# A transformer block on one core: gate and up of token tile 14 computed inside tile 15's attention, and the tail's chain in another order

## The chip, the cores and the metric

The kernel runs on 1 core of one Trainium2 chip, as one program. The metric is the device time of one execution in microseconds (us); a kernel's time is the median of several runs. The engines are named as in the profile: PE (TensorE matmul) with PEld (its weight load), DVE (VectorE), ACT (ScalarE), POOL (GpSimd) and SP (SyncE, which issues nearly all DMAs). Each engine works through its own list of instructions in order and waits at semaphores.

## The reference

```python
def _A_ref(x, wqkv, wo):                       # B, S, D = 1, 2048, 512; H = 32 heads of Dh = 16
    qkv = (x @ wqkv).reshape(B, S, 3, H, Dh)...
    scores = jnp.einsum('bhqd,bhkd->bhqk', q, k) * Dh ** (-0.5)
    p = _softmax(scores, axis=-1)
    o = jnp.einsum('bhqk,bhkd->bhqd', p, v)
    return o.transpose(...).reshape(B, S, D) @ wo
def _B_ref(x, w_gate, w_up, w_down):           # F = 1792
    return _gelu(x @ w_gate) * (x @ w_up) @ w_down
mod = (_silu(c) @ w_mod).reshape(c.shape[0], 6, 1, -1)
sa, ca, ga, sb, cb, gb = ...
h = _layernorm(x) * (1 + ca) + sa
x = x + ga * _A_ref(h, A_wqkv, A_wo)
h = _layernorm(x) * (1 + cb) + sb
x = x + gb * _B_ref(h, B_w_gate, B_w_up, B_w_down)
```

Inputs and output are bf16. The scores are 32 x 2048 x 2048, which makes the exponential the largest elementwise work.

## The kernel before, in words

The 2048 tokens are 16 tiles of 128. As queries they come in seven sets (`SETS`): two of 512 tokens, three of 256, and the last two of one tile each, tile 14 (`SETS[5]`) and tile 15 (`SETS[6]`). The 32 heads are eight quads (`qd`) of four. A unit is one set and one quad; for tiles 14 and 15 the first `QS` quads (5 before) are one unit of 256 queries for both tiles, the others are units of 128 queries for each tile alone, all of tile 14's first. A unit is worked through in rounds of four slots, one slot being 512 columns of scores of one head; there are 2048 slots in all.

The score matmuls (`qk`, `ps_sc<-qT,kme` or `kmo`) fill three PSUM banks at a time, in two alternating groups. ACT takes two or three banks at once through the exponential (`E<-ps_sc 128x1024` or `128x1536`). At times DVE takes one bank of a group instead (`bits`): it computes the exponential by bit work, a first step out of PSUM for each slot and three steps for each round of four slots (`power_task`: `mant`, `square`, `expo`, on 128x2048). Then `pv_mms` accumulates probabilities times values in the bank `ps_pv`; the values have a column of ones, which gives the softmax's sum.

At a unit's end (`unit_end`) DVE copies the accumulator to `osb`. The sums take one of two ways. By the DMA route they go through DRAM (`scr_den`), come back as `den`, DVE takes the reciprocal (`rden`), which goes out (`scr_rec`) and comes back spread over the partitions in four DMAs (`rb`). By `near_end` PE spreads the sums with a matmul against `self32` (`ps_mi<-osb,self` or `ps_sc<-osb,self`) and DVE takes the reciprocal of 128x128 in place. Either way DVE multiplies `onorm<-osb,rb`. Quads 6 and 7 of tiles 14 and 15 take the second way before the change.

Everything else is side work in PE's gaps: projections, then for each set `side_wo` (eight matmuls with `wo`, residual sum, statistics), the norm steps (`ln2_steps`) and `side_ffn` (transposes, gate, gelu, up, product, down). While the exponentials run, a side matmul with 128 columns of weights is issued as four pieces of 32 columns (`split`), which run beside one another; in the tail it is whole. The gate is copied raw from PSUM to `hreg` by DVE, and ACT does the gelu later in two long instructions, since a change between exponential and gelu needs a table load each way.

The order is set when the program is built: `stream` walks the slots with a model of the engines and writes a fixed list for each of them; `plan` gives each piece of side work a first slot and a due slot (`DUE`), and `RULES` holds nine numbers for every 128 slots that steer how side work, DVE's slots and filler matmuls (`ps_mi<-xs,ident`, `ps_pv<-xs,nil`, results unused) are put in.

After the last slot comes `tail`. Before the change two generators run in it: `tail_end` for tile 15 (last reciprocal, `wo`, statistics, norm, transposes, then `tail_ffn`), and `tail_ffn` for tile 14, all of its gate, up and down. `tail_ffn` goes by chunks of four blocks of F: gate, gelu on ACT, up, product, and the downs of the chunk before. `side_last` prepares tile 14 during tile 15's attention, up to the transposes of its normed tokens (`begin=True`). `down_fin` multiplies with `gb`, adds the residual and issues the output's DMA.

Of the kernel before, what the change touches and what calls it, by code (L numbers as in the profile page):

```python
# [6 lines left out]
ACT = mybir.ActivationFunctionType  # L7
ALU = mybir.AluOpType
# [6 lines left out]
P = 128  # L15
# [6 lines left out]
NDC = D // P  # L22
NFC = F // P
# [5 lines left out]
SETS = ((0, 512), (512, 512), (1024, 256), (1280, 256), (1536, 256), (1792, 128), (1920, 128))  # L29
OCOL = (0, 0, 0, 256, 0, 256, 384)  # L30
BCOL = (0, 0, 0, 0, 0, 0, 128)
NSET = len(SETS)
QS = 5
CH = 3
SC = 2 * CH
NSL = 27
# [6 lines left out]
FIRST = 0  # L43
LAST = 3
FLOW = 4
DUE = lambda ends: (ends[1] + 30, 1420, 1605, ends[4] + 10, ends[5] - 20)
URGENT = 12
LATE = 2
RULES = (
# [16 lines left out]
)  # L66
END = (0, None)

# [380 lines left out]
class _Kernel(_Recorder):  # L449
# [12 lines left out]
    def alloc(self):  # L462
# [6 lines left out]
        self.hT = hreg[:, :].rearrange("p (a n) -> p a n", a=NDC)  # L469
        self.prodT = hreg[:, 0:NFC * 512].rearrange("p (f n) -> p f n", f=NFC)  # L470
        self.prodL = hreg[:, 0:NFC * 256].rearrange("p (f n) -> p f n", f=NFC)
        self.tb2 = hreg[:, 0:4 * D].rearrange("p (t n) -> p t n", t=4)
        wreg = sb("wreg", [P, NDC * 1536], BF16)
        self.wqkv = wreg[:, :].rearrange("p (a n) -> p a n", a=NDC)
# [563 lines left out]
        self.done(("ffn", gi))  # L1038


    def side_last(self, k):
        sums = self.near_end(k + 1, 6, self.mi[:, 0:P])
        for y in self.side_ffn(k, True):
            yield y
            if y is END and sums is not None and ("osb", k + 1, 6) in self.have:
                yield from sums
                sums = None
        if sums is not None:
            yield from sums

    def task(self, steps, key, when=None):

# [49 lines left out]
    def plan(self, ends, nsplit):  # L1102

        def at(i):
            return i * 2.5 if i < nsplit / 2.5 else nsplit + 3 * (i - nsplit / 2.5)
        a = ends[0]
        w = [(lambda: self.side_v(0, 0), 0, at(3)), (self.side_first, 0, at(30))]
        w.append((self.side_wo_load, at(30), at(30)))
        w.append((lambda: self.side_dc(1), at(30), at(51)))
        w.append((self.side_mod, at(50), at(59)))  # L1110
        w.append((lambda: self.side_dc(2), at(59), at(90)))
        w.append((lambda: self.side_q_all(1), at(90), at(105)))
        w.append((lambda: self.side_dc(3), at(105), at(133)))
        w.append((lambda: self.side_q_all(2), at(133), at(160)))
        w.append((lambda: self.side_q_all(3), at(160), a + 40))
        n = ends[-1]
        due = DUE(ends)
        for k, e in enumerate(due):
            s0 = max(ends[k] + 33, due[k - 1] if k else 0)
            w.append((lambda k=k: self.side_wo(k), s0, min(e, s0 + 15 * SETS[k][1] // P)))  # L1120
            w.append((lambda k=k: self.side_ffn(k), s0, e))
        k, s0 = len(SETS) - 2, ends[-2] - 16
        w.append((lambda: self.near_end(k, 6, self.mi[:, 0:P]), s0, s0))
        w.append((lambda: self.near_end(k, 7, self.mi[:, 0:P]), s0, s0))
        w.append((lambda: self.side_wo(k), s0, s0))
        w.append((lambda: self.side_last(k), s0, n - 20))
        res = []
        for mk, s, e in w:
            self.dry = True
            tot = sum(y[0] for y in mk() if y is not None)  # L1130
            self.dry = False
            res.append([mk(), s, e, tot, None])
        return res
# [423 lines left out]
    def unit_end(self, u, acc):  # L1557
        sets, qd, q0, W = u
# [1 line left out]
        osb, rb = self.osb[:, lo:hi], self.rb[:, lo:hi]  # L1560
        assert not self.blocked(u)
        self.copy("dve", osb, acc[:, 0:W])
        if sets[0] >= len(SETS) - 2 and len(sets) == 1 and qd >= 6:
            self.done(("osb", sets[0], qd))
            return
        self.live[u] = (lo, hi)
# [32 lines left out]
    def tail(self, ka, kb):  # L1599

        self.split = False
        gens = [self.tail_end(kb), self.tail_ffn(ka, self.pv[:, :], range(0, 3), 0)]
        nxt = [None] * len(gens)
        while True:
            t = self.pe_now()
            while any(self.step(x, max(self.free[x], t) + 40) for x in ("act", "dve", "sp")):
                pass
            best = None
            for i, g in enumerate(gens):
                if g is None:  # L1610
                    continue
                if nxt[i] is None:
                    nxt[i] = next(g, 0)
                if nxt[i] == 0:
                    gens[i] = None
                elif nxt[i] is not None:
                    x = self.probe(nxt[i])
                    if best is None or max(x, t + 30) < best[0]:
                        best = max(x, t + 30), i
# [15 lines left out]
            f, nxt[best[1]] = nxt[best[1]], None  # L1635
            f()

    def tail_end(self, k):
        q0, W = SETS[k]
# [16 lines left out]
        for h in range(2):  # L1656
            pb = self.scp[:, 4 + h, :]
            yield lambda h=h, pb=pb: self.transp(pb, lambda t: self.normed(k, t), 1, h)
            for i in range(2):
                dc = 2 * h + i  # L1660
                self.modulate("act" if i == 0 else "dve", self.t2T[:, dc, c0:c0 + W],
                              pb.bitcast(BF16)[:, W * i:W * i + W], self.modB, dc)
        yield from self.tail_ffn(k, self.mi[:, :], (4, 5, 0, 1, 2, 3), 4)

    def tail_ffn(self, k, down, banks, e0):
        q0, W = SETS[k]
        c0, tile, kpb = BCOL[k], q0 // P, 512 // W
        chunks = [range(a, min(NFC, a + kpb)) for a in range(0, NFC, kpb)]
        nb = [0]

        def up(ci, w):
            if nb[0] == 2 and k == len(SETS) - 1:
                yield from self.until(("p", k - 1, len(chunks) - 1))
            bk = self.scp[:, banks[nb[0] % len(banks)], :]
            nb[0] += 1
            for s, fc in enumerate(chunks[ci]):
                for dci in range(NDC):
                    yield lambda s=s, fc=fc, dci=dci: self.up_mm(bk[:, W * s:W * s + W], w, fc, c0, W, dci)
            return bk
        if k < len(SETS) - 1:  # L1680
            yield from self.until(("begun", k))
            self.act(self.tcol[:, 0:1], self.tcol[:, 0:1], ACT.Gelu_apprx_tanh)
        for ci in range(len(chunks) + 1):
            if ci < len(chunks):
                n = len(chunks[ci])
                g = self.E[:, e0 + ci, 0:W * n]
                bg = yield from up(ci, self.wg)
                self.task([("act", lambda bg=bg, g=g, n=n: self.act(g, bg[:, 0:W * n], ACT.Gelu_apprx_tanh))],
                          ("g", k, ci))
                bu = yield from up(ci, self.wu)  # L1690
                yield from self.until(("g", k, ci))
                self.task([lambda bu=bu, g=g, n=n, f0=chunks[ci][0]: self.stt(
                    self.prodL[:, f0:f0 + n, c0:c0 + W], bu[:, 0:W * n].rearrange("p (k n) -> p k n", k=n), 1.0,
                    g.rearrange("p (k n) -> p k n", k=n), ALU.mult, ALU.mult)], ("p", k, ci))
            if ci:
                yield from self.until(("p", k, ci - 1))
                for fc in chunks[ci - 1]:
# [46 lines left out]
```

## Time and profile before

| | |
|---|---|
| time, median of 3 runs (lowest, highest) | 823.86 us (823.32, 823.99) |
| profiled execution | span 822.1 us from the first to the last instruction; it has no time of its own beside the span |
| ACT busy | 792.7 us, 96% |
| PE busy | 755.0 us, 92% |
| DVE busy | 753.1 us, 92% |
| granted TensorE clock, mean | 1.000 |
| DMA | 43.73 MB, 53 GB/s on the mean |

An engine's busy time is the union of its instructions' times. Matmuls are pipelined and their ends are modelled, so for their rate the distance from one group's start to the next is used, not the mean of one. In the rows of instructions in order the first number is the start and the second the length in us; a bracket at the end gives the idle time before and what ended it. In the rows by group the number behind the bar is busy time in us, then the mean of one instruction in ns, then idle time ahead of the group.

### The profile page before, as it was taken

How to read it: one execution, taken by the hardware profiler on the slowest of the kernel's cores; microseconds unless marked ns; L12 is line 12 of the kernel's file. 1: busy time of each engine (PE TensorE's matmuls, PEld its weight loads, DVE VectorE, ACT ScalarE, POOL GpSimd, SP SyncE). 2: the span in 40 equal slices, each digit the busy share in tenths (PEclk: the TensorE clock that was granted, in tenths of full speed). 3: DMA queues.
4: the chain of work that ended last, by engine and by line, in shares of the span. 5: the costliest groups of instructions: out<-in, count | busy, mean ns of one | idle time of the engine just before them, and what ended most of it. 6: DMA issues, size and time to landing. Idle time of an engine off the chain costs nothing.

```text
span 822.1 us, 30036 instructions
## 1 busy us (share of the span) xinstructions
PE 755.0 (92%) x13614; PEld 296.8 (36%) x13614; DVE 753.1 (92%) x1349; ACT 792.7 (96%) x740; POOL 4.5 (1%) x13
## 2 busy tenths in 40 slices
PE   8999999988898998999898989998899998999998
PEld 3333333322222222222233333333443344345556
DVE  7866999999999999999999999999999999689864
ACT  5999999999999999999999999999999999999982
POOL 2000000000000000000000000000000000000000
PEclk9999999999999999999999999999999999999999
DMA  8101000000003211110002322200644243420000
GB/s 273 63 2 36 9 10 10 10 10 7 4 10 98 59 47 33 46 32 22 16 20 59 87 59 57 54 26 13 174 136 123 73 124 89 126 57 10 22 7 14
DMA packets 76361, 43.73 MB, mean 53 GB/s; under 512 B 20557, under 2 KB 74634, under 8 KB 76234
## 3 DMA queue, kind: packets, MB, share of 16 engines
q1 hardware_dynamic: 76232, 41.82, 18.5%
q8 instruction: 106, 1.74, 0.9%
q14 instruction: 21, 0.17, 0.1%
q10 hardware_dynamic: 2, 0.00, 0.0%
HBM read 39.18 MB, written 2.61 MB: 51 GB/s over the span
## 4 chain that ended last, share of the span: by engine, by line
ACT 90%; PE 6%; DVE 2%; DMA 0%; issue 0%; DVEq 0%
ACT E L356 86%; PE ps_sc L337 4%; ACT hreg L356 3%; PE ps_mi L337 2%; ACT L356 1%; PE ps_pv L337 1%; DVE dreg L368 0%; DMA xs<-in_A_x_dram 0%; DVE hreg L360 0%; DVE st L396 0%; DVE mreg L368 0%; DVE wreg L360 0%; PE ps_sc L341 0%; DVE mreg L360 0%; DVE dreg L360 0%
## 5 line engine op out<-in xcount | busy, mean ns | idle before, releaser
L356 ACT ACTIVATE E<-ps_sc 128x1024 bf16<-128x1024 f32 (+2 forms) x702 | 748.2, 1295 | 11.8 <-PE ps_sc L337 11.8
L337 PE MATMUL ps_sc<-qT,kmo 32*128 32x256 bf16 (+2 forms) x1664 | 199.6, 299 | 20.7 <-ACT E L356 18.2
L337 PE MATMUL ps_sc<-qT,kme 32*128 32x256 bf16 (+2 forms) x1600 | 194.7, 304 | 23.7 <-ACT E L356 19.0
L368 DVE TENSOR_SCALAR mreg<-ps_sc 128x512 uint16<-128x512 f32 x248 | 166.3, 685 | 18.1 <-PE ps_sc L337 15.9
L337 PE MATMUL ps_pv<-E,vaug 128*17 128x256 bf16 (+2 forms) x2536 | 149.4, 300 | 0.5 <-DVE osb L377 0.2
L368 DVE TENSOR_SCALAR dreg<-ps_sc 128x512 uint16<-128x512 f32 x164 | 109.9, 684 | 4.8 <-PE ps_sc L337 3.4
L337 PE MATMUL ps_mi<-wreg,mreg 128*32 128x256 bf16 (+1 forms) x1888 | 108.3, 326 | 4.7 <-DVE hreg L360 2.0
L337 PEld LDWEIGHTS ps_sc<-qT,kme 32*128 32x128 bf16 x1600 | 53.6, 92 | 143.2 <-ACT E L356 120.9
L337 PEld LDWEIGHTS ps_sc<-qT,kmo 32*128 32x128 bf16 x1664 | 56.7, 92 | 129.5 <-ACT E L356 109.8
L337 PEld LDWEIGHTS ps_pv<-E,vaug 128*17 128x17 bf16 x2536 | 51.3, 89 | 55.6 <-issue 40.9
L368 DVE TENSOR_SCALAR mreg<-mreg 128x2048 uint16<-128x2048 uint16 x103 | 69.6, 680 | 0.2
L337 PEld LDWEIGHTS ps_mi<-wreg,mreg 128*32 128x32 bf16 x1888 | 41.0, 95 | 46.6 <-issue 19.5
L337 PE MATMUL ps_pv<-mreg,vaug 128*17 128x256 bf16 (+2 forms) x888 | 51.8, 298 | 3.4 <-DVE mreg L360 1.8
L360 DVE TENSOR_TENSOR mreg<-mreg 128x2048 bf16<-128x2048 bf16 x41 | 49.6, 1211 | 0.0
L360 DVE TENSOR_TENSOR mreg<-dreg,mreg 128x2048 bf16<-128x2048 bf16 x35 | 42.5, 1213 | 0.1
L337 PE MATMUL ps_mi<-hreg,wreg 128*32 128x512 bf16 x480 | 38.5, 384 | 1.1 <-DVE vaug L377 0.9
L360 DVE TENSOR_TENSOR hreg<-ps_mi,hreg 128x512 bf16<-128x512 f32 x47 | 32.2, 684 | 1.3 <-PE ps_mi L337 0.9
L337 PE MATMUL ps_mi<-xs,ident 128*32 128x512 bf16 (+2 forms) x416 | 32.6, 375 | 0.3 <-DVE hreg L360 0.2
L377 DVE CAST hreg<-ps_mi 128x512 bf16<-128x512 f32 x46 | 31.5, 684 | 0.7 <-PE ps_mi L337 0.2
L368 DVE TENSOR_SCALAR dreg<-dreg 128x2048 uint16<-128x2048 uint16 x47 | 32.0, 681 | 0.1
L337 PE MATMUL ps_mi<-wo,onorm 128*32 128x512 bf16 x416 | 31.7, 383 | 0.2 <-DVE qT L368 0.2
L337 PE MATMUL ps_mi<-mreg,hreg 128*32 128x512 bf16 x352 | 28.8, 384 | 0.0
(166 smaller groups left out, 680.1 us busy)
## 6 DMA issues: line engine op xcount, KB each, us to landing
mreg<-in_B_w_up_dram SPq DMA_DIRECT2D x32, 256.0 KB, 3.0
mreg<-in_B_w_gate_dram SPq DMA_DIRECT2D x28, 256.0 KB, 3.7
mreg<-in_B_w_down_dram SPq DMA_DIRECT2D x16, 256.0 KB, 3.0
dreg<-in_B_w_down_dram SPq DMA_DIRECT2D x12, 256.0 KB, 3.4
mreg<-in_w_mod_dram SPq DMA_DIRECT2D x1, 2048.0 KB, 12.7
rb<-scr_rec SPq DMA_DIRECT2D x64, 32.0 KB, 1.9
out_dram<-xs SPq DMA_DIRECT2D x16, 128.0 KB, 1.7
rb<-scr_rec SPq DMA_DIRECT2D x116, 16.0 KB, 1.8
```

Source lines behind the costliest of these rows:

```text
L337: return self.rec("pe", lambda e: e.matmul(out, lhsT, rhs, start=start, stop=stop, tile_position=tp), [lhsT, rhs, *after], [out], cost=(n, ...
L356: return self.rec("act", lambda e: e.activation(out, in_, func, scale=scale, **kw), rd, wr, cost=self.cost("act", out, [in_], "act") + load)
L360: return self.rec(eng, lambda e: e.tensor_tensor(out, a, b, op), [a, b], [out], cost=self.cost(eng, out, [a, b], "tt"))
L368: return self.rec(eng, lambda e: e.tensor_scalar(out, a, s1, s2, **kw), rd, [out], cost=self.cost(eng, out, [a], "ts") + (60 if len(rd) > ...
L377: return self.rec(eng, lambda e: e.tensor_copy(out, in_), [in_], [out], cost=self.cost(eng, out, [in_], "ts"))
```

## The change

`QS` falls to 2, so quads 2 to 7 of tiles 14 and 15 are single units. Quads 6 and 7 of tile 14 and now 5, 6 and 7 of tile 15 go by `near_end` (`PEN`). `side_last` goes on after the transposes with `side_raw`: all eight chunks of tile 14's gate and up are computed inside tile 15's attention and copied raw to `gate5` and `up5` in `hreg`. In the tail, `tail_rest` does tile 14's gelus (ACT, SBUF to SBUF), products and downs; the last two products wait for tile 15's norm. `tail_ffn`, now for tile 15 alone, does all gate chunks first, then up chunks with downs between them. The windows of side work (`WIN`, `DUE`) and ten rows of `RULES` have other numbers, so the built order differs from the last part of the 256-query sets on; ahead of slot 1000 or so it is the same.

```diff
-QS = 5
+QS = 2
+PEN = {NSET - 2: (6, 7), NSET - 1: (5, 6, 7)}
+NRAW = 8
...
-DUE = lambda ends: (ends[1] + 30, 1420, 1605, ends[4] + 10, ends[5] - 20)
+DUE = (1054, 1420, 1597, 1802, -12, 0, -20)
+def WIN(ends):
+    due = DUE[:4] + (ends[5] + DUE[4], ends[5] - 16 + DUE[5], ends[6] + DUE[6])
...
+        self.gate5 = hreg[:, 0:NFC * 256].rearrange("p (f n) -> p f n", f=NFC)[:, :, 0:P]
+        self.up5 = hreg[:, NFC * 256 + 2048:NFC * 256 + 2048 + NFC * P].rearrange("p (f n) -> p f n", f=NFC)
...
+    def raw_chunk(self, k, i, mi):
+        W, c0 = SETS[k][1], BCOL[k]
+        x, f0 = i // 4, i % 4 * 4
+        n = min(4, NFC - f0)
+        for s in range(n):
+            for dci in range(NDC):
+                yield W, lambda s=s, dci=dci: self.up_mm(
+                    mi[:, W * s:W * s + W], (self.wg, self.wu)[x], f0 + s, c0, W, dci)
+        dst = (self.gate5, self.up5)[x][:, f0:f0 + n, :]
+        return lambda eng: self.copy(eng, dst, mi[:, 0:W * n].rearrange("p (k n) -> p k n", k=n))
...
     def side_last(self, k):
-        sums = self.near_end(k + 1, 6, self.mi[:, 0:P])
-        for y in self.side_ffn(k, True):
+        sums = [(qd, self.near_end(k + 1, qd, self.mi[:, 0:P])) for qd in PEN[k + 1][:-1]]
+        for gen in (self.side_ffn(k, True), self.side_raw(k)):
...
-        if sets[0] >= len(SETS) - 2 and len(sets) == 1 and qd >= 6:
+        if len(sets) == 1 and qd in PEN.get(sets[0], ()):
...
-        gens = [self.tail_end(kb), self.tail_ffn(ka, self.pv[:, :], range(0, 3), 0)]
+        gens = [self.tail_end(kb), self.tail_rest(ka, self.pv[:, :])]
...
+    def tail_rest(self, k, down):
...
+        early, late = self.after([("onorm", last, 7)]), self.after([("ln2", last)])
+        when = (early, early, late, late)
+        for j, h in enumerate(part):
...
+            self.task([("act", lambda h=h: self.act(self.gate5[:, h, :], self.gate5[:, h, :], ACT.Gelu_apprx_tanh))], ("g5", j))
+        for j, h in enumerate(part):
...
+            self.task([lambda h=h: self.tt("dve", self.gate5[:, h, :], self.gate5[:, h, :], self.up5[:, h, :], ALU.mult)],
+                      ("p5", j), when[j])
+            yield from self.until(("p5", j))
+            for fc in range(h.start, h.stop):
+                yield lambda fc=fc: self.down_mm(down, BCOL[k] // P, fc)
+        self.task([lambda: self.down_fin(down, q0 // P)], ("fin", k), self.after([("ln2", k + 1)]))
...
-        yield from self.tail_ffn(k, self.mi[:, :], (4, 5, 0, 1, 2, 3), 4)
+        yield from self.tail_ffn(k, self.mi[:, :], (0, 1, 2, 3, 4, 5), 4)
...
+        for i in range(nc):
+            n = len(chunks[i])
+            yield from up(i, self.wg)
...
+        for i in range(nc + 1):
+            if i < nc:
+                n = len(chunks[i])
+                yield from self.until(("g", k, i))
+                yield from up(nc + i, self.wu)
...
+            if i:
+                yield from self.until(("p", k, i - 1))
+                for fc in chunks[i - 1]:
                     yield lambda fc=fc: self.down_mm(down, c0 // P, fc)
```

More of the change, by code (lines that the diff above doesn't have):

```diff
@@ L45 @@
 FLOW = 4
-DUE = lambda ends: (ends[1] + 30, 1420, 1605, ends[4] + 10, ends[5] - 20)
+DUE = (1054, 1420, 1597, 1802, -12, 0, -20)
+def WIN(ends):
+    due = DUE[:4] + (ends[5] + DUE[4], ends[5] - 16 + DUE[5], ends[6] + DUE[6])
+    res = []
+    for k in range(NSET - 2):
+        s0 = max(ends[k] + 33, due[k - 1] if k else 0)
+        res += [(s0, min(due[k], s0 + 15 * SETS[k][1] // P)), (s0, due[k])]
+    return res + [(due[5], due[5]), (due[5], due[6])]
 URGENT = 12
@@ L1038, in side_ffn, with side_raw @@
         self.done(("ffn", gi))
-    def side_last(self, k):
-        sums = self.near_end(k + 1, 6, self.mi[:, 0:P])
-        for y in self.side_ffn(k, True):
[L1044 to L1049, printed above, removed]
+    def raw_chunk(self, k, i, mi):
[8 more added lines that the diff above has]
+        return lambda eng: self.copy(eng, dst, mi[:, 0:W * n].rearrange("p (k n) -> p k n", k=n))
+    def side_raw(self, k):
+        for i in range(NRAW):
+            f = yield from self.raw_chunk(k, i, self.bank())
+            f("dve")
+            self.done(("raw", k, i))
+            yield END
+    def side_last(self, k):
+        sums = [(qd, self.near_end(k + 1, qd, self.mi[:, 0:P])) for qd in PEN[k + 1][:-1]]
+        for gen in (self.side_ffn(k, True), self.side_raw(k)):
+            for y in gen:
+                yield y
+                if y is END and sums and ("osb", k + 1, sums[0][0]) in self.have:
+                    yield from sums.pop(0)[1]
+        for _, x in sums:
+            yield from x
     def task(self, steps, key, when=None):
@@ L1116, in plan @@
         n = ends[-1]
[L1117 to L1126, printed above, removed]
+        win = WIN(ends)
+        for k in range(NSET - 2):
+            w.append((lambda k=k: self.side_wo(k),) + win[2 * k])
+            w.append((lambda k=k: self.side_ffn(k),) + win[2 * k + 1])
+        k = NSET - 2
+        for qd in PEN[k]:
+            w.append((lambda qd=qd: self.near_end(k, qd, self.mi[:, 0:P]),) + win[2 * k])
+        w.append((lambda: self.side_wo(k),) + win[2 * k])
+        w.append((lambda: self.side_last(k),) + win[2 * k + 1])
         res = []
@@ L1617, in tail @@
                     x = self.probe(nxt[i])
-                    if best is None or max(x, t + 30) < best[0]:
-                        best = max(x, t + 30), i
+                    x = max(x, t + 30), i if ("ln2", kb) not in self.have else -i
+                    if best is None or x < best[:2]:
+                        best = x + (i,)
             w = self.next_side()
@@ L1634, in tail @@
                 continue
-            f, nxt[best[1]] = nxt[best[1]], None
+            f, nxt[best[2]] = nxt[best[2]], None
             f()
+    def tail_rest(self, k, down):
+        q0, W = SETS[k]
+        for i in range(NRAW, 8):
+            gen = self.raw_chunk(k, i, self.scp[:, i % 3, :])
+            while True:
+                try:
+                    yield next(gen)[1]
+                except StopIteration as stop:
+                    f = stop.value
+                    break
+            self.task([lambda f=f: f("dve")], ("raw", k, i))
+        part = [slice(a, min(a + 4, NFC)) for a in range(0, NFC, 4)]
+        last = k + 1
+        early, late = self.after([("onorm", last, 7)]), self.after([("ln2", last)])
+        when = (early, early, late, late)
+        for j, h in enumerate(part):
+            for i in range(h.start // 4, (h.stop + 3) // 4):
+                yield from self.until(("raw", k, i))
+            self.task([("act", lambda h=h: self.act(self.gate5[:, h, :], self.gate5[:, h, :], ACT.Gelu_apprx_tanh))], ("g5", j))
+        for j, h in enumerate(part):
+            for i in range(h.start // 4, (h.stop + 3) // 4):
+                yield from self.until(("raw", k, 4 + i))
+            yield from self.until(("g5", j))
+            self.task([lambda h=h: self.tt("dve", self.gate5[:, h, :], self.gate5[:, h, :], self.up5[:, h, :], ALU.mult)],
[4 more added lines that the diff above has]
+        self.task([lambda: self.down_fin(down, q0 // P)], ("fin", k), self.after([("ln2", k + 1)]))
     def tail_end(self, k):
@@ L1668, in tail_ffn @@
         chunks = [range(a, min(NFC, a + kpb)) for a in range(0, NFC, kpb)]
[L1669 to L1676, printed above, removed]
-                for dci in range(NDC):
-                    yield lambda s=s, fc=fc, dci=dci: self.up_mm(bk[:, W * s:W * s + W], w, fc, c0, W, dci)
-            return bk
@@ L1680, in tail_ffn @@
[L1680 to L1697, printed above, removed]
+        nc = len(chunks)
@@ new lines, in tail_ffn, with up @@
+        bank = [self.scp[:, banks[i % len(banks)], :] for i in range(2 * nc)]
+        def up(i, w):
+            for s, fc in enumerate(chunks[i % nc]):
+                for dci in range(NDC):
+                    yield lambda s=s, fc=fc, dci=dci: self.up_mm(bank[i][:, W * s:W * s + W], w, fc, c0, W, dci)
+        for i in range(nc):
+            n = len(chunks[i])
+            yield from up(i, self.wg)
+            g = self.E[:, e0 + i, 0:W * n]
+            self.task([("act", lambda i=i, g=g, n=n: self.act(g, bank[i][:, 0:W * n], ACT.Gelu_apprx_tanh))], ("g", k, i))
@@ new lines, in tail_ffn @@
+        for i in range(nc + 1):
[3 more added lines that the diff above has]
+                yield from up(nc + i, self.wu)
+                g = self.E[:, e0 + i, 0:W * n]
+                self.task([lambda i=i, g=g, n=n: self.stt(
+                    self.prodL[:, chunks[i][0]:chunks[i][0] + n, c0:c0 + W], bank[nc + i][:, 0:W * n].rearrange("p (k n) -> p k n", k=n), 1.0,
+                    g.rearrange("p (k n) -> p k n", k=n), ALU.mult, ALU.mult)], ("p", k, i))
+            if i:
+                yield from self.until(("p", k, i - 1))
+                for fc in chunks[i - 1]:
```

18 rows, old and new, of the table RULES are left out of this document.

## The prediction

> **What bounds the kernel now.** I read the page first, for the shares and the chain of work that ended last.
>
> ```profile
> span 822.1 us, 30036 instructions
> PE 755.0 (92%) x13614; PEld 296.8 (36%) x13614; DVE 753.1 (92%) x1349; ACT 792.7 (96%) x740; POOL 4.5 (1%) x13
> ...
> ACT 90%; PE 6%; DVE 2%; DMA 0%; issue 0%; DVEq 0%
> ```
>
> ACT carries 90% of the chain. The profiled execution has no time of its own beside its span of 822.1; the three runs have a median of 823.86, so 1.76 us lie around the span, and I carry those over unchanged. Where ACT lets go shows in the busy time by stretches and in ACT's timeline.
>
> ```profile
> 20.00:796.30 776.30, 716.63 (x13140) 271.95 (x13132) 724.89 (x1269) 774.56 (x712) 0.31 (x1) 1.00 0.18 49
> 748.90:796.30 47.40, 44.45 (x1327) 25.22 (x1323) 39.28 (x75) 47.38 (x46) 0.00 (x0) 1.00 0.07 15
> 796.27:822.10 25.83, 22.13 (x284) 17.08 (x284) 13.83 (x33) 7.13 (x13) 0.00 (x0) 1.00 0.04 13
> ```
> ```profile
> 748.89 47.36 ACT L356 ACTIVATE E<-ps_sc 128x1024 bf16<-128x1024 f32 x45
> 796.27 1.28 ACT L356 ACT_TABLE_LOAD   x1
> 797.56 0.20 ACT L356 ACTIVATE tcol<-tcol 128x1 f32<-128x1 f32 x1
> ```
>
> The columns after the length are PE, PEld, DVE, ACT, POOL, granted clock, DMA share and GB/s. From 20 to 796.3 ACT is idle for only 1.74 us: exps end to end. At 796.27 the last exp ends, and 25.83 us of tail follow, in which PE is busy for 22.13. So the kernel is "sum of ACT until the last exp" plus "tail", and the change is costed in these two.
>
> **The exps.** Their prices, from the last stretch by form:
>
> ```profile
> L356 ACT ACTIVATE E<-ps_sc 128x1024 bf16<-128x1024 f32 x29 | 28.8, 1122 | 0.0
> L356 ACT ACTIVATE E<-ps_sc 128x1536 bf16<-128x1536 f32 x15 | 22.4, 1565 | 0.0
> ```
>
> The means overlap one another (29 x 1122 alone is 32.5), so I use them only for the difference: 1565 - 1122 = 443 ns for 512 more columns, where one wide exp's overlap may differ from a narrow one's; I take 0.425, and 0.443 moves the sum by under 0.1. Of the 45 exps in 47.36 one is of 512 columns. Then 45 exps in 47.36 give (47.36 - 14 x 0.425) / 45 = 0.920 for 1024 columns, 1.345 for 1536, 0.495 for 512. The instruction lists of the two programs have 444 exps of 1024 before and 451 after, 249 and 246 of 1536, one and none of 512 (tail gelus not counted): DVE takes 408 of the 2048 score slots after, 412 before, because it now has other work. ACT's sum rises by 7 x 0.920 - 3 x 1.345 - 0.495 = **+1.9 us**. The gelu pairs and table loads ahead of the tail are as many as before. With 1.74 us of idle in 776, nothing absorbs this; it moves the last exp.
>
> **PE and DVE under the exps.** Gate and up of tile 14 (SETS[5]) are 112 matmuls of 128 columns; in the attention each is cut into four pieces for 32 columns of weights, 448 pieces, four abreast. Narrow work of that kind, and what PE has to spare in the last stretch:
>
> ```profile
> 786.19 0.40 PE L337 MATMUL ps_pv<-E,vaug 128*17 128x128 bf16 x16
> 786.41 0.40 PE L337 MATMUL ps_pv<-dreg,vaug 128*17 128x128 bf16 x16
> 793.10 0.62 PE L337 MATMUL ps_pv<-mreg,vaug 128*17 128x128 bf16 x32
> 793.66 0.40 PE L337 MATMUL ps_sc<-qT,kmo 32*128 32x128 bf16 x12
> ```
> ```profile
> L337 PE MATMUL ps_mi<-xs,ident 128*32 128x512 bf16 x24 | 2.2, 382 | 0.0
> L337 PE MATMUL ps_pv<-xs,nil 128*17 128x128 bf16 x52 | 1.1, 220 | 0.0
> L337 PE MATMUL ps_pv<-E,vaug 128*17 128x128 bf16 x291 | 7.1, 220 | 0.1
> L337 PE MATMUL ps_pv<-E,vaug 128*17 128x256 bf16 x56 | 2.4, 274 | 0.0
> ```
>
> Sixteen pieces take 0.22 (786.19 to 786.41), so 448 take 6.2; with the switch to score matmuls included, 32 take 0.56, so 7.8 at the worst. QS falls from 5 to 2, so three quads of heads run 128 wide instead of 256: by busy time per column PV costs 7.1/(291x128) = 0.19 ns against 2.4/(56x256) = 0.17, which on 49152 columns is 1.1 us. PE thus needs 7.3 us more. It has 2.95 idle in these 47.4 us and 3.3 of fillers in the two rows above (matmuls whose result is not used): 6.3, and the last tile's own attention starts earlier than 748.9 now, because six of its eight quads are single, before three. The instruction list agrees: single-width nil fillers fall from 52 to 4. I count no loss, but the cover is thin; without it every microsecond goes straight into the exps.
>
> DVE gets eight copies of raw gate and up out of PSUM and loses four score slots and one quad's bit work:
>
> ```profile
> L368 DVE TENSOR_SCALAR mreg<-ps_sc 128x512 uint16<-128x512 f32 x12 | 8.2, 687 | 3.3 <-PE ps_sc L337 3.2
> L368 DVE TENSOR_SCALAR mreg<-mreg 128x2048 uint16<-128x2048 uint16 x7 | 4.8, 681 | 0.1
> L360 DVE TENSOR_TENSOR mreg<-mreg 128x2048 bf16<-128x2048 bf16 x3 | 3.7, 1220 | 0.0
> ```
>
> Six full copies and two halves are about 6 x 0.69 + 2 x 0.42 = 5.0; the loss is 4 x 0.69 + 2 x 0.68 + 1.22 = 5.3. That is even, and DVE has 8 us idle in the last stretch. Two more units go by the DMA route for their reciprocals, 14 more issues on SP, which is idle between them.
>
> **The tail.** Here is the chain of tile 15 (SETS[6]) before, in order of time.
>
> ```profile
> 796.73 0.29 DVE L377 COPY osb<-ps_pv 128x128 f32<-128x128 f32 x1 [0.17 <-PE ps_pv L337]
> ...
> 797.15 0.96 DVE L380 RECIPROCAL rb<-ps_mi 128x128 f32<-128x128 f32 x1
> 797.17 0.44 PE L337 MATMUL ps_sc<-osb,self 128*128 128x128 f32 x2
> ...
> 798.64 0.95 DVE L380 RECIPROCAL rb<-ps_sc 128x128 f32<-128x128 f32 x1
> ...
> 801.23 0.28 DVE L360 TENSOR_TENSOR onorm<-osb,rb 128x128 bf16<-128x128 f32 x1
> ...
> 802.04 0.81 PE L337 MATMUL ps_sc<-wo,onorm 128*128 128x512 bf16 x3
> ...
> 802.89 0.70 DVE L396 BATCH_NORM_STATS2 st<-ps_sc 128x6 f32<-128x512 f32 x1 [1.38 <-PE ps_sc L337]
> ...
> 803.72 0.67 DVE L373 SCALAR_TENSOR_TENSOR hreg<-ps_sc,E 128x512 bf16<-128x512 f32 x1
> ...
> 805.58 0.81 DVE L368 TENSOR_SCALAR E<-ps_sc,mv,rstd 128x512 bf16<-128x512 f32 x1
> ...
> 806.44 0.40 PE L341 MATMUL ps_sc<-ident,E 128*128 128x128 bf16 x4
> ...
> 807.73 1.25 PE L337 MATMUL ps_sc<-wreg,qT 128*128 128x128 bf16 x16
> 808.82 1.06 PE L337 MATMUL ps_sc<-wreg,mreg 128*128 128x128 bf16 x16
> ...
> 811.50 1.03 PE L337 MATMUL ps_mi<-xs,hreg 128*128 128x512 bf16 x4
> ...
> 812.36 1.06 PE L337 MATMUL ps_sc<-wreg,qT 128*128 128x128 bf16 x16
> ...
> 817.40 0.69 DVE L360 TENSOR_TENSOR wreg<-ps_mi,gb 128x512 bf16<-128x512 f32 x1 [0.83 <-PE ps_mi L337]
> ...
> 819.38 0.42 DVE L360 TENSOR_TENSOR xs<-xs,wreg 128x512 bf16<-128x512 bf16 x1
> ```
>
> Three delays stand in it. The last quad's reciprocal starts at 798.64 though its sum was ready at 797.61: quad 6's reciprocal (797.15) was ahead in DVE's queue. Quad 5's onorm came only at 801.23, by the DMA route, so wo waited until 802.04. And PE did tile 14's matmuls in between. After the change quads 5, 6 and 7 of the last tile all go over PE, quad 6's reciprocal is issued ahead of the last osb copy, and tile 14 keeps only gelus, products and its 14 downs.
>
> I lay out the changed order with these durations, in us after the last exp's end. osb copy 0.46 to 0.75 (796.73). Sum on PE to 1.34 (797.61). Reciprocal, at once now, 1.37 to 2.32. onorm to 2.64. One wo matmul, the seven others done: to about 3.15. Stats from 3.19. From stats to norm the old chain took 805.58 - 802.89 = 2.69, with a 0.67 product in it; now a 0.42 one (the nearest row is the bf16 product from SBUF at 819.38; at worst 0.67 as it was): 2.44, so norm 5.63 to 6.44. Transposes to 6.9. Four downs of tile 14 stand in PE's queue ahead of the gate: from 6.95 for 0.86. **Gate starts at 7.8**; before, at 11.46 (807.73).
>
> From there PE has the 112 matmuls of tile 15 (0.89 for sixteen: three groups stand from 808.82 to 811.50), 6.2, and 16 downs (0.86 for four, 811.50 to 812.36), 3.4. The output starts when the last down is through, at 17.5 after the last exp; before, at 21.1 (817.40). No wait is seen in that stretch: while a product is made, PE has the next up chunk or four downs. The output takes 0.69 for the product and 0.42 for the add, 1.2 with the gap; before, tile 14's came behind it, and the last add ended at 819.80, 23.53 after the last exp. Now at 18.7. The last DMA's 2.3 (819.80 to 822.1) stays. The tail shrinks by **4.8 us**, to 21.0. Bounds: 1.2 if only the second output goes, 6.2 if all the moved matmuls do; I take 4.8, as each step but one has its own row.
>
> [...] The row first: the table load is 1.28 long, and the next activation starts at 797.56, 1.29 after it; the first raw gelu, taken at the 0.5 of an exp of 512 columns, is then done at 1.8, well ahead of its product at 2.64. [...]
>
> **Sum.** 823.86 + 1.9 - 4.8 = **821.0**.
>
> **Rivals.** (a) *The chain does not get short.* In DVE's queue quad 4's onorm, by the DMA route, now stands ahead of quad 6's onorm and quad 7's reciprocal. The route, measured:
>
> ```profile
> 794.16 0.34 SPq L406 DMA_DIRECT2D scr_rec<-rden  x1
> 796.43 1.71 SPq L406 DMA_DIRECT2D rb<-scr_rec  x4
> ```
>
> From the reciprocal to the landing is 4.0 us; on SP it stands behind the same steps of quads 2 and 3, which wait for DVE as well. It decides once quad 4's reciprocal runs later than 3.3 us before the last exp's end. In the order eight exps follow it, 8 us, which speaks against; DVE's queue, with eight copies that wait for PE, speaks for. A delay of 2.5 gives 823.5: no change. Chance 0.17.
>
> (b) *PE becomes the bound in the last tile's attention: slower.* If the fillers stood where nothing else can, only the 2.95 idle covers, and the 448 pieces cost 7.8 with switches, PV 1.1 more: 8.9 - 2.95 = 5.9 us of ACT waits, 826.9. It gets slower than before once these waits pass 2.9 us. For it: PE was busy for 94% of that stretch. Against: ACT never waited there (idle 0.0 in all three exp rows). Chance 0.11.
>
> (c) *The clock falls in the tail*, which loses PE work. Every row shows 1.00; at half, the stretch from gate to last down takes 9.7 more: 830.7. [...] Chance 0.04.
>
> That the change does not do what it says is out: all 448 pieces stand ahead of the last score matmuls in PE's list.
>
> **Numbers.** Forecast 0.68, (a) 0.17, (b) 0.11, (c) 0.04. A difference of 0.2%, 1.65 us, is about what a measurement of this kernel can tell from none. Faster is the forecast, 0.68; same is (a), 0.17; slower is (b) and (c), 0.15. The range: low, a tail shorter by 6.2 with all of the 1.9 paid, 819.6, and 0.3 for ACT's share in the rounding of the prices, 819.3; high, the forecast with half of the 6.3 of cover missing, 3.2 more, 824.2, which also holds (a). Left out are (b) and (c), 0.15.
>
> **What would show it.** Right: the last exp ends near 798.2 with ACT idle under 3 us ahead of it, gate starts about 8 us after it, one output at the end, span about 819.2. Wrong on the exps: ACT waits for PE in the last 50 us. Wrong on the tail: an onorm that waits for a DMA, or PE waiting between up and down.

## The result, and the profile after

The changed kernel takes 829.75 us (median of 4, 827.44 to 830.77) against 823.69 before: slower, ratio 1.007 with a 95% interval of 1.0053 to 1.0087. In a second series it was 828.25, ratio 1.005 (1.0032 to 1.0068). The forecast was 821.0, in a range of 819.3 to 824.2. The profiled execution is the fastest of the first four: 827.44, span 825.7, with a mean clock of 1.000, where the three others had 0.994 to 0.998.

First the page of the changed kernel, then ACT's instructions in order at the end of the attention.

```profile
span 825.7 us, 31347 instructions
PE 753.6 (91%) x14256; PEld 303.8 (37%) x14256; DVE 754.5 (91%) x1359; ACT 795.3 (96%) x742; POOL 4.5 (1%) x13
...
q8 instruction: 111, 1.82, 0.9%
...
ACT 83%; PE 11%; DVE 2%; DMA 1%; SPq 1%; issue 1%; DVEq 0%
```
```profile
782.97 4.37 ACT L369 ACTIVATE E<-ps_sc 128x1024 bf16<-128x1024 f32 x4
788.24 2.46 ACT L369 ACTIVATE E<-ps_sc 128x1024 bf16<-128x1024 f32 x2 [0.91 <-PE ps_sc L350]
791.54 1.02 ACT L369 ACTIVATE E<-ps_sc 128x1024 bf16<-128x1024 f32 x1 [0.84 <-PE ps_sc L350]
792.77 1.45 ACT L369 ACTIVATE E<-ps_sc 128x1536 bf16<-128x1536 f32 x1 [0.21 <-PE ps_sc L350]
795.29 2.46 ACT L369 ACTIVATE E<-ps_sc 128x1024 bf16<-128x1024 f32 x2 [1.07 <-PE ps_sc L350]
799.03 3.38 ACT L369 ACTIVATE E<-ps_sc 128x1024 bf16<-128x1024 f32 x3 [1.28 <-PE ps_sc L350]
803.22 1.02 ACT L369 ACTIVATE E<-ps_sc 128x1024 bf16<-128x1024 f32 x1 [0.82 <-PE ps_sc L350]
804.26 1.28 ACT L369 ACT_TABLE_LOAD   x1
805.56 1.97 ACT L369 ACTIVATE hreg<-hreg 128x512 bf16<-128x512 bf16 x4
```

PE's share of the chain went from 6% to 11%. The last exp ends at 804.26; before it was 796.27, the forecast 798.2. The brackets say what ACT did in between: six waits for score matmuls in 20 us, 5.1 us in all. The tail behind the last exp is 825.7 - 804.26 = 21.4 us, against 25.8 before and 21.0 forecast. So the tail came out nearly as worked out, and the exps did not.

What PE did meanwhile, by the same stretch of 20.3 us ahead of the last exp's end, in the changed kernel and in the one before (columns: PE, PEld, DVE, ACT, POOL, clock, DMA share, GB/s):

```profile
784.00:804.30 20.30, 15.48 (x720) 11.79 (x711) 10.69 (x21) 15.16 (x15) 0.00 (x0) 1.00 0.05 10
```
```profile
776.00:796.30 20.30, 18.93 (x613) 11.09 (x607) 13.93 (x33) 20.28 (x21) 0.00 (x0) 1.00 0.07 10
```

ACT waits for PE, and yet PE is busy for less of these 20.3 us than before: 15.48 against 18.93. So its array is not full here. PE's own instructions in order, around its five stops:

```profile
785.59 0.85 PE L350 MATMUL ps_mi<-wreg,qT 128*32 128x128 bf16 x47
787.42 0.34 PE L350 MATMUL ps_mi<-wreg,qT 128*32 128x128 bf16 x9 [0.97 <-issue]
...
789.92 0.28 PE L350 MATMUL ps_sc<-qT,kme 32*128 32x128 bf16 x3
791.17 0.34 PE L350 MATMUL ps_sc<-qT,kme 32*128 32x128 bf16 x5 [0.97 <-issue]
...
793.00 0.62 PE L350 MATMUL ps_mi<-wreg,mreg 128*32 128x128 bf16 x31
794.63 0.29 PE L350 MATMUL ps_mi<-wreg,mreg 128*32 128x128 bf16 x5 [1.02 <-issue]
...
798.66 0.34 PE L350 MATMUL ps_sc<-qT,kmo 32*128 32x128 bf16 x5 [1.24 <-issue]
...
802.40 0.23 PE L350 MATMUL ps_pv<-dreg,vaug 128*17 128x128 bf16 x3 [0.56 <-issue]
```

PE stops for 0.6 to 1.2 us in the middle of runs of like matmuls; "issue" means that no semaphore or engine explains the stop. Counted in PE's instruction list, the stops stand ahead of matmuls 13496, 13624, 13752, 13880 and 14008: exactly 128 apart (a float32 matmul counts twice: the five sums of `near_end` have ten records), and a matmul has one weight load with it (14256 of each on the page), so every 256 instructions. From restart to restart it is 3.75, 3.46, 4.03 and 3.74 us, 29.3 ns a matmul on the mean, though pieces cost 13.8 ns of array time (between the stops the raw pieces start 13 to 14 ns apart). The page's row of instruction transfers has 1.82 MB in 111 packets, 16.4 KB each; 111 blocks of 256 are 28416 instructions, and PE's matmuls and loads are 2 x 14256 = 28512.

The trace also has the times of these packets on queue q8, and they settle what PE waits for. Times are in us:

| packet begins | packet ends | PE restarts |
|---|---|---|
| 785.16 | 786.09 | 787.42 |
| 788.57 | 789.79 | 791.17 |
| 792.29 | 793.25 | 794.63 |
| 795.78 | 797.23 | 798.66 |
| 799.81 | 801.05 | 802.40 |

Each restart comes 1.3 to 1.4 us after a packet has ended, however long the packet took (0.9 to 1.5 us), and the next packet begins 1.1 to 1.2 us after the restart. These three times add up to the distance from restart to restart: each time the next transfer began only after PE had gone on.

**Theory S** (supply): PE's instructions arrive in blocks of 256, where several blocks follow one another about one in 3.7 us, and the 448 pieces with their loads asked for more. As an estimate, 720 matmuls at 29.3 ns are 21.1 us, for which ACT has 15.2 us of exps: 5.9 short, 5.1 measured. The 29.3 ns come from this same stretch, so that sum is no test of its own. Before, 613 at 29.3 are 18.0 us, and 20.3 were there. **Rival A**: PE's array was full, rival (b) as the prediction worked it. **Rival W**: PE waits for data, such as the banks that DVE's raw copies free.

### The profile page after: what moved, and what is told of

Same layout as the page of the kernel before. It is cut to its first block, busy times and chain, and to the rows that moved or that the text cites. A ratio compares the mean times of both kernels' runs of the same rounds, so it can differ in the third digit from the quotient of the medians.

```text
span 825.7 us, 31347 instructions
## 1 busy us (share of the span) xinstructions
PE 753.6 (91%) x14256; PEld 303.8 (37%) x14256; DVE 754.5 (91%) x1359; ACT 795.3 (96%) x742; POOL 4.5 (1%) x13
## 3 DMA queue, kind: packets, MB, share of 16 engines
q8 instruction: 111, 1.82, 0.9%
## 4 chain that ended last, share of the span: by engine, by line
ACT 83%; PE 11%; DVE 2%; DMA 1%; SPq 1%; issue 1%; DVEq 0%
ACT E L369 80%; PE ps_sc L350 6%; PE ps_mi L350 3%; ACT hreg L369 2%; PE ps_pv L350 1%; ACT L369 1%; SPq L419 1%; DMA xs<-in_A_x_dram 1%; DVE mreg L381 0%; DMA rb<-scr_rec 0%; DVE hreg L373 0%; DVE wreg L373 0%; DVE wreg L381 0%; DVE mreg L373 0%; DVE osb L390 0%
## 5 line engine op out<-in xcount | busy, mean ns | idle before, releaser
L369 ACT ACTIVATE E<-ps_sc 128x1024 bf16<-128x1024 f32 (+1 forms) x701 | 749.0, 1292 | 10.7 <-PE ps_sc L350 10.4
L350 PE MATMUL ps_sc<-qT,kmo 32*128 32x256 bf16 (+2 forms) x1728 | 199.2, 294 | 21.4 <-ACT E L369 17.8
L381 DVE TENSOR_SCALAR mreg<-ps_sc 128x512 uint16<-128x512 f32 x256 | 171.3, 686 | 11.9 <-PE ps_sc L350 9.9
L350 PE MATMUL ps_mi<-wreg,mreg 128*32 128x256 bf16 (+2 forms) x1888 | 107.2, 325 | 4.9 <-DVE hreg L373 1.2
L350 PEld LDWEIGHTS ps_sc<-qT,kme 32*128 32x128 bf16 x1728 | 57.8, 92 | 142.4 <-ACT E L369 115.8
L381 DVE TENSOR_SCALAR dreg<-ps_sc 128x512 uint16<-128x512 f32 x152 | 102.1, 686 | 3.1 <-PE ps_sc L350 1.7
L381 DVE TENSOR_SCALAR mreg<-mreg 128x2048 uint16<-128x2048 uint16 x96 | 65.0, 682 | 0.1
L373 DVE TENSOR_TENSOR dreg<-mreg,dreg 128x2048 bf16<-128x2048 bf16 x32 | 38.9, 1216 | 0.1
L373 DVE TENSOR_TENSOR mreg<-mreg 128x2048 bf16<-128x2048 bf16 x32 | 38.8, 1212 | 0.0
L390 DVE CAST hreg<-ps_mi 128x512 bf16<-128x512 f32 (+1 forms) x50 | 33.8, 675 | 4.4 <-PE ps_mi L350 3.9
L350 PE MATMUL ps_pv<-dreg,vaug 128*17 128x256 bf16 (+2 forms) x528 | 29.7, 290 | 3.0 <-DVE dreg L373 1.8
```

Of the source, the lines that this page charges most:

```text
L350: return self.rec("pe", lambda e: e.matmul(out, lhsT, rhs, start=start, stop=stop, tile_position=tp), [lhsT, rhs, *after], [out], cost=(n, ...
L369: return self.rec("act", lambda e: e.activation(out, in_, func, scale=scale, **kw), rd, wr, cost=self.cost("act", out, [in_], "act") + load)
L373: return self.rec(eng, lambda e: e.tensor_tensor(out, a, b, op), [a, b], [out], cost=self.cost(eng, out, [a, b], "tt"))
L381: return self.rec(eng, lambda e: e.tensor_scalar(out, a, s1, s2, **kw), rd, [out], cost=self.cost(eng, out, [a], "ts") + (60 if len(rd) > ...
L390: return self.rec(eng, lambda e: e.tensor_copy(out, in_), [in_], [out], cost=self.cost(eng, out, [in_], "ts"))
```

## The experiments

**The raw matmuls whole.**

```diff
-    def up_mm(self, bank, w, fc, c0, W, dci):
-        self.mm(..., start=(dci == 0), stop=(dci == NDC - 1))
+    def up_mm(self, bank, w, fc, c0, W, dci, whole=False):
+        self.mm(..., start=(dci == 0), stop=(dci == NDC - 1), whole=whole)
...
-                    mi[:, W * s:W * s + W], (self.wg, self.wu)[x], f0 + s, c0, W, dci)
+                    mi[:, W * s:W * s + W], (self.wg, self.wu)[x], f0 + s, c0, W, dci, True)
```

> The changed kernel with one edit: the 112 raw gate and up matmuls of tile 14 are issued whole (128 columns of weights), not as 448 pieces of 32 columns. Array time is nearly the same (112 x 0.056 = 6.2 us against 448 x 0.0138 = 6.2); 336 matmuls and as many weight loads fewer in PE's list, everything else as planned before. Theory S (PE's instruction supply: in the last 17 us of the attention PE stops for about 1 us exactly every 128 matmuls, so 128 matmul and load pairs take 3.4 to 4.0 us however short they are): the stops vanish, ACT waits for PE after 690 us fall from 6.4 to under 2 us, the last exp ends at 798 to 800, time 821 to 824. Rival A (PE's array is full, as in rival (b) of the prediction): the array time is the same, so are the waits; 827 to 830. Rival W (PE waits for data: DVE's raw copies free the banks too late): same copies, same waits; 827 to 830.

Measured 822.82 (820.62 to 828.32, 10 runs), ratio to the kernel before 0.9993 (0.9976 to 1.0011). Its waits between 690 and 799 us, ACT's end and PE's last 15 us of attention:

```profile
ACT E L369 <- PE ps_sc L350: 1.1, 2, 0.8
```
```profile
798.93 1.28 ACT L369 ACT_TABLE_LOAD   x1
```
```profile
784.00:798.90 14.90, 14.50 (x355) 1.00 0.07 10
```

In the last 20 us no stop is left, ACT waits for 1.1 us from 690 us on, and the last exp ends at 798.9. (One stop of 0.31 us at 755.0, ahead of matmul 12472, stands here too; in the changed kernel it is 0.41 us.) The array time is that of the changed kernel (whole ones start 56 to 57 ns apart; in groups of 28 and more, four pieces take 52 to 55 ns), and so are DVE's copies, so rivals A and W fall: 336 matmuls less in the list took back some 6 us.

**More instructions in the kernel before.**

```diff
+                for h in range(2 if q0 == SETS[-1][0] else 1):
...
+            if q0 == SETS[-1][0] and not (last and kk == kpb - 1):
+                self.nil_mm(acc[:, 0:16], self.xs[:, NT - 1, 0:16], VW)
```

> The kernel before the change, with more instructions on PE and hardly more array time, in the three single units of tile 15 (its last 22 us of attention): each score matmul of 128 columns is issued as two of 64, and after each four PV matmuls come four with zero weights on 16 columns. 384 score matmuls in place of 192, 228 zero ones more, 16 filler matmuls fewer: about 400 more matmuls. The result is unchanged. Theory S: 520 matmuls in the last 20 us become about 900, at 3.4 to 4.0 us for 128 that is 24 to 28 us: stops of about 1 us appear, ACT waits 3 to 8 us, time 827 to 832. Rival A: score columns are the same, the zero matmuls have 228 x 16 columns, 0.4 us, less 0.6 us of fillers: time 823 to 825.

Measured 832.56 (831.93 to 834.15), ratio 1.0109 (1.0094 to 1.0124). Its waits from 690 to 808, two of its stops (the first line is what ran ahead of the first stop), and PE in three stretches (PE, clock, DMA share, GB/s):

```profile
ACT E L356 <- PE ps_sc L337: 10.1, 10, 2.6
```
```profile
784.85 0.22 PE L337 MATMUL ps_pv<-E,vaug 128*17 128x128 bf16 x4
786.68 0.19 PE L337 MATMUL ps_pv<-xs,nil 128*17 128x16 bf16 x4 [1.61 <-issue]
...
801.11 0.28 PE L337 MATMUL ps_sc<-qT,kmo 32*128 32x64 bf16 x8 [1.39 <-issue]
```
```profile
774.00:786.50 12.50, 10.00 (x416) 1.00 0.08 17
786.50:796.80 10.30, 9.87 (x332) 0.50 0.03 7
796.80:803.40 6.60, 5.18 (x274) 1.00 0.05 9
```

The longest wait, 2.6 us, lies in the tail; ahead of the last exp ACT waits for 7.5 us, within the 3 to 8 that theory S expected, and the time is 0.6 above its range. With hardly more array time the old kernel gets the same stops and 8.7 us more. They stand at matmul 12857 of its own list and at multiples of 128 from there, which is 57 modulo 128; those of the changed kernel are at 56. The list's few instructions that are no matmul or load, 80 ahead of the stops here and 82 there, make up for the difference: counted in, all of these stops stand at instruction 194 modulo 256. The phase is the list's, not the work's. The clock is new here: from a stop of 1.61 us on PE ran at half speed for 10 us, so not all of the 8.7 is supply.

**A half dose, and none**: `NRAW = 4` and `NRAW = 0` in the changed kernel.

> The changed kernel with NRAW = 4: the gate of tile 14 in the attention (224 pieces), its up in the tail. A half dose. Theory S: 224 pieces less is about 1.75 blocks of 128 less, at 3.7 us a block against the 3.1 us of their array time: waits after 690 us fall from 6.4 to 1 to 3 us; the tail gets 56 whole matmuls, 3.1 us, part of it in gaps: 22 to 24.5; time 823 to 827. Rival A: waits fall by at most the 3.1 us of array time, to over 3 us, time 826 to 829.

> The changed kernel with NRAW = 0: no gate or up matmul of tile 14 in the attention, all of them in the tail; QS = 2, the three quads over PE and the new tail order stay. Tells what the rest of the change does alone. Theory S: without the 448 pieces PE's list is thin enough, ACT waits after 690 us under 2 us, last exp at 798 to 800; the tail gets 112 whole matmuls (6.2 us) and eight copies back, of which some lies in the chain's gaps: tail 24 to 27 us; time 824 to 828. Rival A (the 128-wide units of QS = 2 themselves are what fills PE): waits of 4 us or more remain, time 828 to 832.

`NRAW = 4`: 826.57 (826.18 to 828.34), ratio 1.0034 (1.0022 to 1.0046); waits of ACT 3.4 us in the same window, with three stops left:

```profile
ACT E L369 <- PE ps_sc L350: 3.4, 5, 1.1
```
```profile
787.11 0.34 PE L350 MATMUL ps_mi<-wreg,qT 128*32 128x128 bf16 x9 [1.18 <-issue]
...
790.86 0.34 PE L350 MATMUL ps_sc<-qT,kme 32*128 32x128 bf16 x5 [0.97 <-issue]
```

The first is ahead of the same matmul, 13496, as with the full dose. The waits miss the top of the expectation by 0.4. Both they and the time also lie in what rival A expected, so this run does not part the two. `NRAW = 0`: 826.06 (825.14 to 827.05), ratio 1.0026 (1.0016 to 1.0037). Its exps run without a stop and end at 743.95 + 53.91 = 797.9, where the sum of ACT (+1.9) had put them:

```profile
743.95 53.91 ACT L369 ACTIVATE E<-ps_sc 128x1024 bf16<-128x1024 f32 x52
```

Its tail is 824.3 - 797.9 = 26.4. So without the moved matmuls the rest of the change costs 2.2 us: the exps it adds, and no shorter tail. Against this run, the move of all 112 matmuls is worth 3.2 us when they are whole (822.82) and loses 2.2 to 3.7 as pieces (828.25 and 829.75).

**The changed kernel once more.**

> The changed kernel as it is, for more executions and a second profile. Its first profile had a granted clock of 1.000 and 827.4 us, three other executions 0.994 to 0.998 and 829.8 to 830.8. Theory S plus clock: the 1 us stops of PE leave a stretch so thin that in most executions the clock falls to half for some us inside the last 17 us of the attention; a profile of 829 us or more then shows a clock under 1 there, and an ACT wait total after 690 us of 8 us or more. Rival: the clock falls only after PE's last matmul, where it costs nothing, and the spread comes from elsewhere (DMA, ACT).

828.25 (826.33 to 829.29). This profile is of a run of 829.29, and its clock fell (PE, clock, DMA share, GB/s):

```profile
794.00:797.00 3.00, 1.43 (x74) 1.00 0.02 6
797.00:800.50 3.50, 3.50 (x113) 0.51 0.04 9
800.50:806.00 5.50, 5.17 (x216) 1.00 0.03 6
```
```profile
797.58 1.02 ACT L369 ACTIVATE E<-ps_sc 128x1024 bf16<-128x1024 f32 x1 [1.78 <-PE ps_sc L350]
...
806.12 1.28 ACT L369 ACT_TABLE_LOAD   x1
```

After a stop in which PE was busy for 1.43 of 3 us it ran at half clock for 3.4 us, and the last exp ended at 806.1, 1.9 later than in the first profile. ACT waited 7.7 us in the window, under the 8 expected. So the clock that rival (c) had in the tail fell too, but inside the attention and right behind a stop. That the stops caused it is the likely reading and not tested alone; that the other executions of 829 us and more have the same is not shown.

**Is whole issue a gain by itself?** A flag `thick` in `mm` issues all side matmuls and fillers whole, from a slot on: `ends[4]` is slot 1792, and the third run has `nsplit`, the end of the first phase, in its place.

```diff
-        if self.split and not whole and tp is None and ...
+        if self.split and not self.thick and not whole and tp is None and ...
...
+            self.thick = pos >= ends[4]
```

> The kernel before the change, with side matmuls and fillers whole from slot 1792 on (12922 matmuls against 13612). Its PE is not short of instructions (ACT waits 0.0 in the last stretch). Theory S: no gain, 823 to 825. If it gains over 1.5 us, whole matmuls are a gain of their own, and the return of the run with only the raw ones whole was not the supply.

> The changed kernel, with every side matmul and filler from slot 1792 on issued whole (the raw gate and up as in the run before, and now also tile 14's wo, the fourth set's gate, up and down, and the fillers): 13299 matmuls against 13917 with only the raw ones whole and 14253 as changed. The planner re-plans, and by its lists ACT has 448 exps of 1024 and 249 of 1536, 1.3 us more than the changed kernel. Theory S: no stops, ACT waits after 690 us under 1 us; last exp at 798.5 to 800; time 820 to 823. Rival (whole matmuls block the array for the score matmuls, which is why they were cut): ACT waits for PE grow, over 825.

> The changed kernel, with side matmuls and fillers whole from the end of the first phase on (10183 matmuls). By the lists ACT's sum is 0.3 us over that of the changed kernel. Theory S: as the run before, no stops at the end, 819 to 823; ahead of the last 20 us PE's list was never the limit, so nothing is gained there. Rival (cut pieces run beside score matmuls of other row groups, whole ones cannot): ACT waits for PE in the earlier stretches too, over 826.

Before the change, from slot 1792 on: 829.41 (829.03 to 829.89), ratio 1.0067 (1.0052 to 1.0082), 5.6 us slower. Changed kernel, from slot 1792 on: 825.67, ratio 1.0025 (1.0015 to 1.0034). From the first phase's end on: 835.46, ratio 1.0143 (1.0122 to 1.0163). All three missed what theory S alone gives. In the first, 4.9 of the 5.6 us are a single wait:

```profile
774.72 26.12 ACT L356 ACTIVATE E<-ps_sc 128x1024 bf16<-128x1024 f32 x26 [4.86 <-PE ps_sc L337]
```

Ahead of these score matmuls PE's list has PV matmuls that wait for DVE's steps of the exponential, so most of this loss belongs to the order that was built, and without it no gain is left either. In the second ACT waits for 2.2 us ahead of the last exp, beside the 1.3 us of exps that its plan adds. In the third the last exp ends at 804.4, and the tail takes 29.3 us, in which ACT waits for DVE's raw copies. None of them shows a gain from whole issue, so the return of the first experiment is not a bonus of whole matmuls. Whether a whole matmul also blocks the array for score matmuls, as the rivals say, stays open.

**A faster version?** From the run with the raw matmuls whole: five fillers in the tail's gaps, and `QS` of 3 and 4.

> The run with the raw matmuls whole, and five filler matmuls of 512 columns into a free bank in the gaps that tile 15's chain leaves on PE in the tail. Its own runs went from 820.6 to 828.3 us, and its profile had the clock fall only behind PE's last matmul. If the spread comes from the clock falling inside the tail, where PE is busy for only about half of 4 us, the fillers hold it: highest run under 824, median 821 to 822.5. If not (the clock falls in the attention, or the spread is elsewhere), spread and median stay, 822 to 824, and the fillers cost up to 0.3.

> The run with the raw matmuls whole, and QS = 3: one more quad for both tiles at once, so 256 columns wide: 128 fewer score and PV matmuls (13809 against 13917 in all, ACT's exps as many). Tile 14 ends later, and by the lists most of the raw up chunks fall behind the last score matmuls, into the tail, some of them ahead of wo on PE. Theory S: no stops; the tail gets up to 56 whole matmuls, 3.1 us, mostly in the chain's gaps (4 us of them): 820.5 to 823.5. If the raw chunks hold up wo and DVE's reciprocal chain, 824 to 826.

> The same with QS = 4: 13705 matmuls, ACT's sum 2.3 us lower than with QS = 2 by the lists (450 exps of 1024, 245 of 1536), and all of the raw gate and up falls behind the last score matmuls, between the steps of tile 15's chain. Theory S and the sum of ACT: last exp 1.5 to 2.5 us earlier than with QS = 2; the tail has 112 whole matmuls, 6.2 us, against about 4 us of gaps, 2 us longer and more if wo waits for them: 821 to 825.

823.49 (821.96 to 826.70), ratio 0.9995 (0.9985 to 1.0006); 823.70, ratio 0.9998 (0.9989 to 1.0007); 831.63, ratio 1.0093 (1.0078 to 1.0109). The fillers did not hold the time under 824, which speaks against the clock in the tail as the cause of the spread; that fillers can hold the clock was the author's estimate and is not shown. Of these two kernels no execution over 823 was profiled, so the cause stays open; with and without the fillers the longest execution, 826.70 and 828.32 us, is the one with the lowest mean clock, 0.996 and 0.994. `QS = 3` is 0.2 above its range. `QS = 4` misses its own by 6.6: the last exp does not end earlier (799.5), ACT waits between the raw gelus, and in the tail the clock is at half for 3.4 us from 801.8 on (0.997 on the mean of that execution), the place that rival (c) had named. None is faster than the kernel before by more than the measurement tells.

## Why the prediction was wrong, point by point

- **The step that failed** is "PE and DVE under the exps", where the 448 pieces were priced by array time and covered by idle time and fillers, with "I count no loss". The cover in array time was there: issued whole, with the same array time, they cost ACT next to nothing. What the pieces cost is their places in the instruction list: 29 ns each with its load instead of 13.8. In the first profile that is 5.1 us of waits in the last 20 us, and the last exp ends 6.1 later than forecast. Of the two earlier waits from 690 us on, one (0.47) stands behind a stop at 754.6 ahead of matmul 12472, and the other (0.76) is in the run without the pieces too. The median lies another 2.3 us above this profiled execution; where they went, no profile of those executions shows.
- **Rival (b)** had the place, the sign and nearly the time (826.9; the profiled run took 827.4), at a chance of 0.11, but for a reason that the runs refute: an array that is full. So the near hit of its number is luck. What spoke "against" it, that ACT never waited before, was weak evidence: PE's list had 613 matmuls in 20.3 us there, 33 ns each, only 13% above the 29 ns of the stretch with the stops.
- **The exps** (+1.9): right. 797.9 without the pieces, 798.2 forecast.
- **The tail** (-4.8): right in mechanism and nearly in size, -4.4. Gate was to start 7.8 after the last exp:

```profile
812.09 0.83 PE L350 MATMUL ps_sc<-wreg,qT 128*128 128x128 bf16 x7
...
822.34 0.69 DVE L373 TENSOR_TENSOR wreg<-ps_mi,gb 128x512 bf16<-128x512 f32 x1 [0.87 <-PE ps_mi L350]
```

  It started at 812.09 - 804.26 = 7.8. The last output's product began at 18.1 instead of 17.5.
- **Rival (a)** did not come: no onorm in the tail waited for a DMA.
- **Rival (c)**: no row ahead of the prediction shows the half clock that its 830.7 is worked with. The runs showed it: 0.50 over 10.3 us with more instructions in the kernel before and 0.51 over 3.5 us in the second profile of the changed kernel, both inside the attention. In the tail `QS = 4` had it for 3.4 us from 801.8 on, right behind the last exp and ahead of the stretch from gate to last down that was to take 9.7 more; the first profile of the changed kernel has 1.00 there. The half and the chance of 0.04 were the author's estimates.
- **The table load**: 804.26 to the first raw gelu at 805.56 is 1.30; before, from 796.27 to 797.56, it was 1.29. The load is 1.28 long, and the gelu begins 0.02 behind its end.
- Even without the stops the forecast is not reached: the whole pieces gave 822.8, not 821.0, and no change by its interval. In its profile the last exp is 0.7 later than forecast, and the tail is 821.0 - 798.9 = 22.1.

## What to carry to other kernels

Work that is moved under another engine's time needs room in two budgets: the array's time (here 13.8 ns a piece), and the rate at which its instructions arrive (here 29.3 ns a matmul with its load, in blocks of 256). Count instructions per microsecond in the stretch that is filled up, loads too, over several blocks of 256, and compare with the densest stretch of that length that the trace shows without a stop. Cutting a matmul into four kept the array time here (52 to 55 ns for four pieces, 56 to 57 for a whole one) and took four times the list (448 pieces for 112). The column of busy time does not show this; a wait put down to "issue" in the middle of like instructions does, and so do the times of the instruction packets.

## What the runs showed of the hardware

PE stopped for 0.2 to 1.6 us at one phase of its list of instructions, 194 modulo 256 (193 for the two at 755), where several blocks of 256 in a row were asked for faster than they came; from restart to restart it was 3.5 to 4.6 us. A single fast block did not stop it: blocks of 3.1 us (before, from 776.6 on) and 3.2 us (after, up to 737.4) passed without. The two short stops at 755 come at the end of slower blocks (5.5 us), behind a packet that began 3.2 us (after) and 2.0 us (whole pieces) into the block; why it began so late stays open. In the first profile the next block's packet began 1.1 to 1.2 us after a restart, took 0.9 to 1.5 us, and PE went on 1.3 to 1.4 us after its end.

Behind two stops of 1.6 us the granted clock was halved, for 3.4 us in one profile and for 10.2 us in another. The longest gaps of PE ahead of these two falls were 1.57 and 1.61 us. In the profile before and in the first one after, no gap of PE is over 1.24 us, and the clock is 1.00 up to its last matmul. How long a gap has to be to bring the clock down, and whether its length alone decides, no run shows.
